# One kept V quarter fewer, and the second MLP split between two places, in a cached-attention decoder on one Trainium2 core

## Chip, cores, metric

The kernel runs on one core of a Trainium2 chip. The metric is the time of one execution in device microseconds, with lower being better. Executions of one kernel spread over about 1.1% here (the kernel before: 1127.4 to 1140.3 us over all rounds; against itself 0.9983 with an interval of 0.996 to 1.0005), so a difference under 0.3% is not told apart by one set of rounds.

## The reference, cut to what matters

There are eight batch rows with one token each. Two layers use the same caches and the same weights.

```python
x = x + _A_ref(_layernorm(x), K, V, wq, wo)      # attention, 16 query heads over 8 K/V heads,
x = x + _B_ref(_layernorm(x), w1, w2, w3, w4)    #   4096 places, 256 wide, in each of 8 rows
x = x + _A_ref(_layernorm(x), K, V, wq, wo)      # again, the same caches
x = x + _B_ref(_layernorm(x), w1, w2, w3, w4)
```

A K or V tile of one row and one head is 2 MB (128 partitions of 16 KB). Read in full for both layers, the 128 K and 128 V tile reads would be 537 MB. The kernel keeps part of a row's K and V on the chip between its two layers. Since the sequence has length one, the shifted parts of `_B_ref` (w1, w2) are zero and what remains is one MLP (w3, w4).

## The kernel before

The program is built from operations with dependencies, and a small list scheduler on the host sets the fixed order of each engine and the place of each load. The tiles are handled in quarters of 512 KB. The buffer has 30 slots of one quarter each.

```python
QUARTERS = 30          # slots of one quarter (4 KB of each partition)
KEEP_K = 5             # heads whose K stays for the second layer: 20 slots
KEEP_V = 4             # quarters of one head's V that stay too
...
def next_kv(i):        # when and where the next load is issued
    ...                # m: 1 to 4 neighbouring quarters of one tile in one load
    late = max(free["sp"], dma_end - self.LEAD)
    ...                # waits for m free neighbouring slots until `late`,
    m = min(m, max(k for k, a in runs(t)))   # then takes what there is
    ...
    q = min(fit) if u.keep else max(fit) + k - m
    return t, m, q
```

The order of work is one loop over the rows. `mid` is the MLP between the two layers of a row; while it runs, the first layer's heads of the next row use their V.

```python
for b in range(B):
    ...
    mid(b, order2[:first])                     # MLP between the layers, queries of layer 2
    run([("b", 0, b + 1, h) ...free heads])    # P.V of the next row's first heads
    if b < B - 2:
        run(both(1, b, order2))                # layer 2 of this row
        run(both(0, b + 1, kept_heads, ...))   # layer 1 of the next row, heads that are kept
    ...
    else:                                      # the last row
        k = both(1, b, l2_heads, ...)
        run(k[:MLP_AT])
        urge[0] = 0
        mlp(x3T[:, :, :], "x3all", B, xoT[:, :, :], ["xo"])   # second MLP, rows 0 to 6, in a batch
        result(B - 1)                                         # their output
        urge[0] = CH
        run(k[MLP_AT:] + ...)
mlp(x1c[B % 2], ("x3", B - 1), 1, xoT[:, :, 0:1], ["xo"])     # second MLP of the last row: the end
result(1)
```

One `mlp` is the sums of the norm, 56 matmuls with w3, 70 with w4, and some 25 small DVE steps.

## Time and profile before

| reading | value |
|---|---|
| time, median of 4 runs | 1131.13 us (1128.87 to 1132.88; 1129.86 of the first 3) |
| span of the first profile | 1124.7 us (a second profile: 1129.4 us) |
| bytes on the load queue | 446.80 MB |
| rate where nothing holds it back | 424 GB/s |
| rate at the turns between rows | 377 to 402 GB/s over 55 us |

I call "turn" the stretch in which a row goes from its first to its second layer. A row's turn is the window from 15 us before to 40 us after DVE writes `x1c` (the row after the first attention), and what it loses is 55 us x (1 - rate / 424 GB/s). The sum over the first seven rows is "the turns' loss" below; the eighth turn is counted by itself, as the last row follows it. (The recorded expectations below quote losses from earlier counts over other windows, such as 28.2 us where this measure gives 24.5; compare them only among themselves.) Here are three of the seven windows, from the stretches of the first profile (columns: window, length, busy time and count of PE, weight loads, DVE, ACT and POOL, granted clock, DMA share, GB/s):

```profile
115.00:170.00 55.00, 45.40 (x1094) 31.50 (x1092) 22.32 (x98) 5.72 (x27) 4.53 (x12) 0.91 1.02 393
...
785.00:840.00 55.00, 45.44 (x1076) 34.18 (x1076) 24.49 (x100) 7.72 (x31) 4.53 (x12) 0.94 0.99 391
918.00:973.00 55.00, 43.38 (x1083) 31.06 (x1083) 23.76 (x100) 7.33 (x33) 4.94 (x13) 1.00 1.00 398
```

The DMA share is near 1 in all of them although the rate is 6 to 8% under the plateau, so the share alone does not show the dip. The rate does.

### The profile page before, as it was taken

How to read it: one execution, taken by the hardware profiler on the slowest of the kernel's cores; microseconds unless marked ns; L12 is line 12 of the kernel's file. 1: busy time of each engine (PE TensorE's matmuls, PEld its weight loads, DVE VectorE, ACT ScalarE, POOL GpSimd, SP SyncE). 2: the span in 40 equal slices, each digit the busy share in tenths (PEclk: the TensorE clock that was granted, in tenths of full speed). 3: DMA queues.
4: the chain of work that ended last, by engine and by line, in shares of the span. 5: the costliest groups of instructions: out<-in, count | busy, mean ns of one | idle time of the engine just before them, and what ended most of it. 6: DMA issues, size and time to landing. Idle time of an engine off the chain costs nothing.

```text
span 1124.7 us, 42351 instructions
## 1 busy us (share of the span) xinstructions
PE 959.9 (85%) x19455; PEld 771.8 (69%) x19455; DVE 556.0 (49%) x1749; ACT 275.8 (25%) x839; POOL 98.0 (9%) x273
## 2 busy tenths in 40 slices
PE   5888888898789989798898987989878988898887
PEld 4677557785678757687677855777666975676775
DVE  4345435455365544454455543655534554456444
ACT  1133012341123302243023411233012430132120
POOL 0001010010100101010010101001010010110010
PEclk9899899899899999999899998899999999999888
DMA  9999999999999999999999999999999999999993
GB/s 334 408 424 421 389 397 424 422 421 382 419 425 423 415 379 422 423 425 408 393 425 423 421 387 409 423 425 420 371 412 426 424 417 374 426 420 398 365 336 132
DMA packets 59570, 449.50 MB, mean 400 GB/s; under 512 B 6384, under 2 KB 9600, under 8 KB 34688
## 3 DMA queue, kind: packets, MB, share of 16 engines
q1 hardware_dynamic: 59392, 446.80, 97.5%
q8 instruction: 152, 2.49, 0.9%
q14 instruction: 26, 0.21, 0.0%
HBM read 446.77 MB, written 0.01 MB: 397 GB/s over the span
## 4 chain that ended last, share of the span: by engine, by line
PE 53%; DMA 35%; DVE 5%; issue 5%; SPq 1%; POOL 0%; ACT 0%
DMA kv<-in_A_k_cache_dram 23%; PE psT L1067 21%; PE psS L915 15%; DMA kv<-in_A_v_cache_dram 11%; PE psP L970 8%; PE psR L1017 3%; PE psM L771 2%; PE psT L1231 1%; DVE oS L982 1%; DVE oS L984 1%; DMA w3x_sb<-in_B_w_dram 1%; PE psP L992 1%; PE psM L868 1%; PE psM L871 1%; SPq L571 1%
## 5 line engine op out<-in xcount | busy, mean ns | idle before, releaser
L1067 PE MATMUL psT<-ident_f,kv 128*128 128x128 f32 x2816 | 398.4, 288 | 32.1 <-DMA kv<-in_A_k_cache_dram 28.9
L1075 DVE COPY kv<-psT 128x512 f32<-128x512 f32 x388 | 267.1, 691 | 214.9 <-PE psT L1067 213.9
L1067 PEld LDWEIGHTS psT<-ident_f,kv 128*128 128x128 f32 x2816 | 320.2, 147 | 54.2 <-DMA kv<-in_A_k_cache_dram 35.4
L1076 ACT COPY kv<-psT 128x512 f32<-128x512 f32 x316 | 184.9, 586 | 407.6 <-PE psT L1067 407.6
L970 PE MATMUL psP<-kv,pT 128*2 128x256 bf16 x4096 | 168.2, 278 | 26.0 <-DMA kv<-in_A_v_cache_dram 15.1
L940 ACT ACTIVATE pT<-sS,nb 128x32 bf16<-128x32 f32 x256 | 81.7, 326 | 332.1 <-DVE nb L934 332.0
L915 PE MATMUL psS<-q2T,kv 128*128 128x48 bf16 x4096 | 141.9, 187 | 20.2 <-issue 19.3
L915 PEld LDWEIGHTS psS<-q2T,kv 128*128 128x128 bf16 x4096 | 126.3, 99 | 44.0 <-issue 39.4
L915 PEld LDWEIGHTS psS<-q1T,kv 128*128 128x128 bf16 x4096 | 136.9, 98 | 14.4 <-issue 9.6
L915 PE MATMUL psS<-q1T,kv 128*128 128x48 bf16 x4096 | 145.7, 184 | 0.9 <-issue 0.9
L970 PEld LDWEIGHTS psP<-kv,pT 128*2 128x2 bf16 x4096 | 79.2, 82 | 63.9 <-issue 25.9
L932 POOL PARTITION_ALL_REDUCE gm<-pm x128 | 45.6, 356 | 792.2 <-DVE pm L930 792.2
L927 DVE COPY sS<-psS 128x64 f32<-128x64 f32 x128 | 28.7, 224 | 120.7 <-PE psS L915 116.3
L992 PE MATMUL psP<-sel,oS 128*128 128x2 bf16 x512 | 32.2, 166 | 48.6 <-DVE oS L984 44.0
L982 DVE CAST oS<-psP 128x256 bf16<-128x256 f32 x128 | 53.9, 421 | 38.7 <-PE psP L970 35.6
L992 PEld LDWEIGHTS psP<-sel,oS 128*128 128x128 bf16 x512 | 24.4, 99 | 68.4 <-DVE oS L984 62.8
L1017 PE MATMUL psR<-wo_sb,oT 128*1 128x448 bf16 x448 | 65.4, 375 | 5.1 <-DVE oT L998 4.9
L944 POOL PARTITION_ALL_REDUCE Db<-rs x128 | 51.2, 400 | 202.2 <-ACT pT L940 202.2
L984 DVE TENSOR_TENSOR oS<-psP,oS 128x256 bf16<-128x256 f32 x128 | 54.2, 423 | 3.2
L1231 PE MATMUL psT<-ident_b 128*128 128x512 bf16 x162 | 54.4, 416 | 0.0
L940 ACT ACTIVATION_READ_ACCUMULATOR pT<-sS,nb 128x1 f32 x256 | 48.1, 188 | 0.0
L771 PEld LDWEIGHTS psM<-x2c,wq_sb 128*128 128x128 bf16 x768 | 30.3, 98 | 21.7 <-issue 17.1
(126 smaller groups left out, 505.7 us busy)
## 6 DMA issues: line engine op xcount, KB each, us to landing
kv<-in_A_k_cache_dram SPq DMA_DIRECT2D x71, 2048.0 KB, 21.7
kv<-in_A_v_cache_dram SPq DMA_DIRECT2D x51, 2048.0 KB, 19.2
kv<-in_A_v_cache_dram SPq DMA_DIRECT2D x171, 512.0 KB, 7.6
kv<-in_A_v_cache_dram SPq DMA_DIRECT2D x42, 1024.0 KB, 12.1
kv<-in_A_k_cache_dram SPq DMA_DIRECT2D x9, 1536.0 KB, 16.0
kv<-in_A_v_cache_dram SPq DMA_DIRECT2D x7, 1536.0 KB, 15.0
kv<-in_A_k_cache_dram SPq DMA_DIRECT2D x21, 512.0 KB, 8.8
kv<-in_A_k_cache_dram SPq DMA_DIRECT2D x10, 1024.0 KB, 14.5
```

The costliest lines, as they stand in the source:

```text
L771: last = t.matmul(bank[:, at + i * step:at + i * step + copies], w, r, start=(kc == 0), stop=(kc == 3))
L915: last = t.matmul(ps[:, 2 * i:2 * i + 2 * REP], a[:, c:256:2], bcast(rhs(c), REP, 1), start=(c == 0), stop=(c == 1))
L940: return a.activation(pT[nr][:, :, :].rearrange("p i j -> p j i")[:, jj, :], sview[:, jj, :], ACT.Exp, bias=nb[nm][:, jj:jj + 1], scale=IN ...
L970: last = t.matmul(ps[g4:g4 + 2, PV0:PV0 + DH], pT[nr][:, i, :], slot_ap(q, s * 256, 256), start=(i < 4), stop=(i >= 28), skip_group_check= ...
L982: plan.op("dve", lambda v: v.tensor_copy(oS[:, 0, :], po), 0.36, "o", rd=[("pv", par, x) for x in range(4)], wr=["oS0"], banks=[bk], prio=hi)
L984: plan.op("dve", lambda v: v.tensor_tensor(oS[:, 1, :], po, oS[:, 0, :], ALU.subtract), 0.36, "o", rd=["oS0"] + [("pv", par, x) for x in r ...
L992: last = t.matmul(ps[:, PV1 + 2 * c:PV1 + 2 * c + 2], oS[:, w, c:DH:2], sel[:, :], start=(w == 0), stop=(w == 1))
L1017: last = t.matmul(psR[r:r + 1, 0:D], oT[no][:, i % 2, i // 2:i // 2 + 1], wo_sb[:, a:a + D], start=(k == 1 and i < 2), stop=(k == HKV - 1 ...
L1067: last = t.transpose(psT[bank][:, s * P:(s + 1) * P], src, ident_f[:, :])
L1075: return e.tensor_copy(dst, psT[bank][:, :])
L1076: return e.copy(dst, psT[bank][:, :])
L1231: return t.matmul(psT[bank][:, :], ident_b[:, :], bcast(ident_b[:, :], 4, 1), start=True, stop=True)
```

## The change

It has four parts: three V quarters kept instead of four, so that one more slot is free while the buffer is fullest; the second MLP of rows 0 to 5 as a batch inside the seventh row's first layer, and that of rows 6 and 7 together at the end; a longer lead from issue to transfer in the scheduler's model; and a placing rule, by which a quarter goes next to the one before it when it fits.

```diff
-KEEP_V = 4
+KEEP_V = 3
-MLP_AT = 3
+MLP_ROW, MLP_AT = 5, 9
-    ISSUE, LEAD = 3.5, 6.0
+    ISSUE, LEAD = 4.0, 6.0
...
+            before = sp_next[i - 1].unit if i else None
+            if before is not None and before.tile is u.tile:
+                for k, a in fit:
+                    if a <= before.slot + 1 <= a + k - m:
+                        return t, m, before.slot + 1
...
+    def with_first_results(k, b):
+        if b != MLP_ROW:
+            return run(k)
+        run(k[:MLP_AT])
+        urge[0] = 0
+        mlp(x3T[:, :, :], "x3all", B - 2, xoT[:, :, 0:B - 2], [("xo", 0)])
+        result(B - 2, 0)
+        urge[0] = CH
+        run(k[MLP_AT:])
...
-            run(k[:MLP_AT])
-            urge[0] = 0
-            mlp(x3T[:, :, :], "x3all", B, xoT[:, :, :], ["xo"])
-            result(B - 1)
-            urge[0] = CH
-            run(k[MLP_AT:] + [("b", 1, b, h) for h in free_heads])
-    mlp(x1c[B % 2], ("x3", B - 1), 1, xoT[:, :, 0:1], ["xo"])
-    result(1)
+            run(k + [("b", 1, b, h) for h in free_heads])
+    mlp(xf, "xf", 2, xoT[:, :, B - 2:B], [("xo", B - 2)])
+    result(2, B - 2)
```

Left out are the lines that make `sums`, `moments`, `norm` and `mlp` take a number of rows. The first output can no longer wait for the end: its row buffer shares bytes with the MLP buffers that later rows need, so the load queue (which is in order) carries it amid the loads.

## The prediction

> **What bounds the kernel now.** I read the slices of the page first, then the queues, then the waits of the load queue, then the stretches.
>
> ```profile
> DMA  9999999999999999999999999999999999999993
> GB/s 334 408 424 421 389 397 424 422 421 382 419 425 423 415 379 422 423 425 408 393 425 423 421 387 409 423 425 420 371 412 426 424 417 374 426 420 398 365 336 132
> ...
> q1 hardware_dynamic: 59392, 446.80, 97.5%
> ```
>
> The DMA row is full, but the GB/s row has two levels: about 424 for most of the time, and a dip to 371-397 once in every batch row, some 130 us apart. The last three slices fall to 365, 336 and 132. So the plateau is the transfer rate, and the kernel loses time where it cannot keep that rate. 446.80 MB at 424 GB/s is 1053.8 us; the span is 1124.7 us, so 70.9 us are lost. To place them I asked for the stretches (columns: window, its length, then busy time and count of PE, weight load, DVE, ACT, POOL; granted clock; DMA share; GB/s).
>
> ```profile
> 0.00:20.00 20.00, 6.62 (x65) 6.16 (x66) 8.01 (x34) 1.28 (x1) 1.18 (x17) 1.00 0.88 353
> 20.00:60.00 40.00, 33.78 (x666) 26.17 (x664) 12.96 (x38) 7.33 (x21) 2.29 (x6) 0.91 1.02 385
> ...
> 829.00:920.00 91.00, 79.67 (x1494) 68.32 (x1493) 47.45 (x126) 30.68 (x87) 9.07 (x24) 0.96 1.01 422
> 880.00:925.00 45.00, 41.72 (x790) 37.03 (x788) 25.16 (x62) 19.86 (x54) 4.94 (x13) 1.00 1.01 421
> 1033.00:1054.00 21.00, 19.02 (x475) 13.12 (x468) 11.90 (x58) 0.22 (x1) 0.00 (x0) 0.84 0.95 354
> 1054.00:1066.00 12.00, 9.12 (x200) 8.70 (x197) 3.97 (x15) 3.20 (x11) 1.51 (x4) 0.86 1.02 398
> 1066.00:1093.00 27.00, 24.12 (x531) 20.20 (x527) 13.84 (x55) 6.01 (x22) 3.02 (x8) 0.81 0.93 317
> 1093.00:1105.00 12.00, 9.04 (x234) 7.13 (x238) 5.09 (x18) 2.61 (x10) 1.51 (x4) 1.00 1.02 416
> 1105.00:1125.00 20.00, 16.13 (x315) 9.71 (x307) 9.17 (x37) 0.22 (x1) 0.00 (x0) 0.79 0.03 11
> ```
>
> The loss of a window is its length times (1 - rate/424). Start: 3.3 + 3.7 = 7.0 us. Last row, 1033 to 1105: 3.5 + 0.7 + 6.8 + 0.2 = 11.2 us. After the last load: about 19.5 us with no traffic, the closing chain. The seven turns between rows, read in the same way from one window each (391 GB/s over 55 us, 397 over 50, 391 over 45, 396 over 45, 396 over 50, 388 over 50, 391 over 45), lose 4.3, 3.2, 3.5, 3.0, 3.3, 4.2 and 3.5: 25.0 us. Together 62.7 of 70.9; the rest is scattered small change in slices of 415 to 422.
>
> Why a turn dips shows in what the load queue waits for, and in its sizes at one turn (780 to 840 us):
>
> ```profile
> SPq L588 <- PE psS L915: 442.6, 102, 25.1
> SPq L588 <- PE psP L970: 424.5, 163, 21.5
> ```
>
> ```profile
> kv<-in_A_v_cache_dram SPq DMA_DIRECT2D x23, 512.0 KB, 8.1
> ```
>
> The queue waits almost always for a matmul of scores or of P·V to give up a quarter of the 30-quarter buffer. At a turn, 20 K quarters and 4 V quarters are kept for the second layer, so 6 are left to stream through: 6 times 524 KB is 3.1 MB in the air or being read. Six windows of 3 us from 793 to 811 us have 350, 381, 306, 391, 300 and 386 GB/s, 352 in the mean; at that rate one pass of a slot takes 3.15 MB / 352 = 8.9 us, of which 8.1 us is the time from issue to landing. The turn is short of slots, not of queue.
>
> **What the Trainium skill says.** "DMA: Bandwidth & Descriptors", Where 436 GB/s comes from, gives a fabric ceiling of 435.2 GB/s; the plateau of 424 agrees (the same page's 358 per core is not what binds here). The same page, Anatomy of one DMA, puts a fixed cost of about 2 us on each DMA (for the other issuing path), mostly the receipt of the last byte: with 1.24 us of transfer per quarter, a lone quarter would need some 3.3 us (an estimate from that page), so most of the 8.1 us here is queueing behind the other quarters; no run shows a lone one yet. "TensorE: Matmul & The Clock Gate", What's actually happening, says that the clock halves after an idle window of about 3.4 us; the trace has 0.50 granted at 1045-1051 and 1075-1081 us, in the last row, so matmul work there costs up to double. "VectorE: DVE Perf Modes", The DRAIN you can't avoid, advises to count instructions, not to fuse; the closing chain's dependent DVE steps do follow one another every 0.20 us at 128x2.
>
> **The change, part by part.**
>
> 1. *Three V quarters kept.* 8 rows each fetch one quarter again: 8 x 0.524 MB = 4.2 MB, at 424 GB/s **+9.9 us** of transfer. In return a turn has 7 streaming slots instead of 6. By the pass time above, 7/6 of 352 is 411 GB/s if a pass stays 8.9 us; a turn's mean of 387 to 397 could thus reach the plateau. But PE too is busy there with the row's MLP and queries, and a slot that waits for a matmul is not helped by a neighbour. Of the 25.0 us of turns plus the 3.5 us of 1033-1054, which is the eighth turn, I take 60% as recovered: **-17.1 us**. This fraction is my choice, and the largest uncertainty.
>
> 2. *The batch leaves the last row.* In its own timeline it is on PE from 1065.1 to 1079.8 us: sums 0.29 + 0.95, first layer 1.47, second layer 0.75 + 0.70 + 1.47, output transposes 0.62, so 6.2 us busy, plus a 1.1 us "issue" gap in the middle of its second layer; DVE adds some 22 small steps of about 0.2 us. The stretch 1066-1093 has PE busy 24.1 of 27 us and only 317 GB/s: here PE, partly at half clock, holds the loads back, which is the 6.8 us loss. Without the batch most of it should go: **-5.5 us**.
>
> 3. *The batch enters the seventh row's first layer* (its place in program order is among the kept heads, around 880-925 us). With 6 rows it has 28 + 56 + 70 + 4 matmuls instead of 36 + 56 + 70 + 4, near 5 us at full clock. PE is busy 41.7 of 45 us there and 79.7 of 91 in the wider stretch, at 421-422 GB/s: it has room for most of 5 us, the loads run 20 us ahead. **+1.5 us**.
>
> 4. *The closing MLP does two rows.* It is the path that sets the end (1114.9 to 1123.2 us). Added: 4 matmuls of sums (0.1), one more variance step (0.2), a second t_h (0.3), a second hidden-layer step (0.25), two base steps (up to 0.2 beside the others), wider gelu steps (0.05). The first layer's 56 matmuls and the second's 70 stay the same in number and width (24 and 12 columns). **+1.1 us**.
>
> 5. *Issue lead 3.5 to 4.0, next quarter next to the last one.* These move only the static order and the placement: more 1-2 MB loads, fewer 512 KB ones. Loads of 512 KB ran at 408-433 GB/s where they were plentiful, so size alone is worth little. **0**, give or take 3.
>
> Sum: 9.9 - 17.1 - 5.5 + 1.5 + 1.1 = -10.1. 1129.9 - 10.1 gives **1120 us**.
>
> **Rivals.** (a) *The slot is not what limits the turn; PE's chain is.* For: PE is 78-85% busy in the seven turn windows and has its gaps there. Against: the queue never stops waiting for slots and 8.1 of 8.9 us are transfer and its queue. Then item 1 recovers perhaps 5 us and the whole is +2: 1132 us. (b) *The first output takes the place of the batch as a wait.* Its row buffer shares bytes with the MLP buffers, and the loads queue is in order, so the output must go out amid the loads (12 places on) and must land before DVE turns the seventh row's sums at about 927 us, as DVE stalls behind that wait. The batch comes some 35 us earlier, so I expect it done; if not, one stall of 5-10 us: 1126-1130. Against it: the order is built with this dependency in view. (c) *The turns close wholly.* Then 28.5 recovered instead of 17.1: 1108 us; the last row's 11.2 then also shrinks to PE's own limit.
>
> **Range and chances.** The recovered share from 20% to 95% gives 1131 to 1110; the last row's 2 to 8 us and the placement's 3 add to both sides. Range 1108 to 1132. Faster by over 2% means below 1107.3, which needs rival (c) and more: 0.07. Slower by over 2% needs 23 us, two stalls of a kind that I do not see: 0.02. Within 2%: 0.91.
>
> **What would show it.** 451.0 MB on the load queue, V issues of 512 KB fewer. Turns at 405-420 GB/s instead of 388-397: item 1; if they stay under 395, rival (a). No sums of eight rows near 1065 us, and the stretch before the last load above 380 GB/s: item 2. The batch's matmuls near 890 us with the rate still at 415 or more, and the turn of the seventh row no later: item 3; a gap on DVE before the cast of the row sums there: rival (b). The end of loads to the end of the kernel 20.5-21.5 us: item 4. The prediction is wrong if the turns stay dipped or if the added traffic is fully paid.

## The result

The changed kernel takes 1131.26 us in the median (1130.45 to 1132.41), the kernel before 1131.13 us in the same rounds; the ratio is 1.0003 with an interval of 0.998 to 1.0026. The record has no mark of correctness for this run itself; `after_keep4` and `after_noadj`, which differ from it by one constant or one rule, are marked correct. Nothing was gained. 10 us of gain had been forecast.

The slices and the load queue of the changed kernel:

```profile
GB/s 342 407 424 421 389 397 426 422 420 382 408 423 424 400 374 420 425 422 415 380 423 424 423 396 399 424 425 420 394 407 425 423 390 385 418 424 414 364 408 153
...
q1 hardware_dynamic: 60544, 450.99, 97.9%
```

The traffic is what was forecast, 451.0 MB, but the dips are all still there. The same three turns in the changed kernel:

```profile
116.00:171.00 55.00, 45.76 (x1040) 28.93 (x1029) 20.11 (x92) 4.64 (x26) 4.12 (x11) 0.84 1.01 394
...
792.00:847.00 55.00, 45.23 (x1058) 30.87 (x1056) 23.81 (x100) 6.56 (x32) 4.92 (x13) 0.91 1.01 400
928.00:983.00 55.00, 44.59 (x1056) 31.54 (x1056) 23.22 (x99) 6.79 (x29) 4.88 (x13) 0.90 1.01 394
```

The turns' loss is 25.2 us in the changed kernel. It is 24.5 us in the first profile of before and 29.4 us in its second, so the first was a lucky one (its span of 1124.7 us is below every timed median too). The load queue still waits for the same two kinds of matmul (waits of the load queue: total, times, longest):

```profile
SPq L596 <- PE psS L947: 467.6, 102, 24.8
SPq L596 <- PE psP L1002: 392.1, 168, 22.4
```

A single-quarter V load of the sixth turn (787 to 847 us) now takes 9.4 us from issue to landing:

```profile
kv<-in_A_v_cache_dram SPq DMA_DIRECT2D x25, 512.0 KB, 9.4
```

The prediction quotes 8.1 us for the corresponding turn of before; the second profile of before has 7.3. Over all seven turns (windows from 20 us before to 40 us after `x1c`), the turns' medians for these loads are 8.4 us in the mean, against 7.6 and 7.4 in the two profiles of before. There is one slot more to six, and the time from issue to landing grew with it. That undoes the arithmetic of the forecast and is the subject of the experiments.

The last row did become shorter. Writes of `x1c` by DVE (start, duration, line, operation, tiles, idle before it) tell the rows apart. In the kernel before, they are the sixth, seventh and eighth row's, the second MLP's input of the last row (the fourth line), and the last copy before the output:

```profile
800.07 0.17 DVE L1051 TENSOR_TENSOR x1c<-acc,psM 128x5 bf16<-128x5 f32 x1 [0.83 <-PE psM L871]
933.17 0.17 DVE L1051 TENSOR_TENSOR x1c<-acc,psM 128x5 bf16<-128x5 f32 x1 [1.01 <-PE psM L871]
1036.36 0.17 DVE L1051 TENSOR_TENSOR x1c<-acc,psM 128x5 bf16<-128x5 f32 x1 [1.26 <-PE psM L871]
1114.65 0.17 DVE L1051 TENSOR_TENSOR x1c<-acc,psM 128x5 bf16<-128x5 f32 x1 [1.32 <-PE psM L871]
1122.83 0.38 DVE L1093 COPY o_row<-psM 1x448 bf16<-1x448 bf16 x1 [0.73 <-PE psM L1089]
```

In the changed kernel the same five, the fourth of which now writes `xf`:

```profile
807.27 0.17 DVE L1083 TENSOR_TENSOR x1c<-acc,psM 128x5 bf16<-128x5 f32 x1 [1.60 <-PE psM L903]
943.26 0.17 DVE L1083 TENSOR_TENSOR x1c<-acc,psM 128x5 bf16<-128x5 f32 x1 [0.83 <-PE psM L903]
1047.20 0.17 DVE L1083 TENSOR_TENSOR x1c<-acc,psM 128x5 bf16<-128x5 f32 x1 [0.85 <-PE psM L903]
1119.15 0.17 DVE L1083 TENSOR_TENSOR xf<-acc,psM 128x5 bf16<-128x5 f32 x1 [0.85 <-PE psM L903]
1128.11 0.38 DVE L1125 COPY o_row<-psM 2x448 bf16<-2x448 bf16 x1 [0.92 <-PE psM L1121]
```

From the eighth row's `x1c` to the end of the span it is 88.4 us before and 82.9 us after. The stretch from the last attention to the copy of the output grew from 8.2 to 9.0 us. The seventh row, from the sixth `x1c` to the seventh, grew from 133.1 to 136.0 us. So the kernel gained at the end and paid earlier: the eighth row's `x1c` comes 10.8 us later than in the first profile of before and 6 us later than in the second (1041.2).

### The profile page after: what moved, and what is told of

It is laid out like the page before. It is cut to its first block, busy times and chain, and to the rows that moved or that the text cites. A ratio compares the mean times of both kernels' runs of the same rounds, so it can differ in the third digit from the quotient of the medians.

```text
span 1130.1 us, 42402 instructions
## 1 busy us (share of the span) xinstructions
PE 971.3 (86%) x19466; PEld 771.2 (68%) x19466; DVE 552.3 (49%) x1749; ACT 278.3 (25%) x844; POOL 97.6 (9%) x275
## 4 chain that ended last, share of the span: by engine, by line
PE 51%; DMA 37%; issue 5%; DVE 5%; POOL 1%; ACT 0%; SPq 0%; POOLq 0%; DVEq 0%
DMA kv<-in_A_k_cache_dram 25%; PE psT L1099 19%; PE psS L947 14%; DMA kv<-in_A_v_cache_dram 13%; PE psP L1002 8%; PE psR L1049 3%; PE psM L797 2%; PE psT L1268 2%; DVE oS L1016 1%; DVE oS L1014 1%; PE psP L1024 1%; PE psM L900 1%; PE psM L903 1%; PE psM L813 1%; ACT pT L972 0%
## 5 line engine op out<-in xcount | busy, mean ns | idle before, releaser
L1099 PE MATMUL psT<-ident_f,kv 128*128 128x128 f32 x2816 | 394.4, 286 | 29.0 <-DMA kv<-in_A_k_cache_dram 27.6
L1107 DVE COPY kv<-psT 128x512 f32<-128x512 f32 x383 | 263.9, 691 | 207.9 <-PE psT L1099 206.5
L1108 ACT COPY kv<-psT 128x512 f32<-128x512 f32 x321 | 188.1, 587 | 416.0 <-PE psT L1099 416.0
L1002 PE MATMUL psP<-kv,pT 128*2 128x256 bf16 x4096 | 181.4, 291 | 19.8 <-DMA kv<-in_A_v_cache_dram 12.5
L972 ACT ACTIVATE pT<-sS,nb 128x32 bf16<-128x32 f32 x256 | 81.9, 327 | 323.5 <-DVE nb L966 323.4
L947 PEld LDWEIGHTS psS<-q1T,kv 128*128 128x128 bf16 x4096 | 136.4, 97 | 14.4 <-issue 10.2
L1268 PE MATMUL psT<-ident_b 128*128 128x512 bf16 x177 | 59.6, 410 | 0.0
L797 PEld LDWEIGHTS psM<-x2c,wq_sb 128*128 128x128 bf16 x768 | 30.3, 98 | 21.5 <-issue 15.8
```

The lines of the kernel that those rows point to most:

```text
L797: last = t.matmul(bank[:, at + i * step:at + i * step + copies], w, r, start=(kc == 0), stop=(kc == 3))
L947: last = t.matmul(ps[:, 2 * i:2 * i + 2 * REP], a[:, c:256:2], bcast(rhs(c), REP, 1), start=(c == 0), stop=(c == 1))
L972: return a.activation(pT[nr][:, :, :].rearrange("p i j -> p j i")[:, jj, :], sview[:, jj, :], ACT.Exp, bias=nb[nm][:, jj:jj + 1], scale=IN ...
L1002: last = t.matmul(ps[g4:g4 + 2, PV0:PV0 + DH], pT[nr][:, i, :], slot_ap(q, s * 256, 256), start=(i < 4), stop=(i >= 28), skip_group_check= ...
L1099: last = t.transpose(psT[bank][:, s * P:(s + 1) * P], src, ident_f[:, :])
L1107: return e.tensor_copy(dst, psT[bank][:, :])
```

## Experiments

The theory after the result (A): the fourth V quarter's traffic, 8 x 0.524 MB at 424 GB/s = 9.9 us, is paid in full, and the seventh slot gives little or nothing at the turns. The rival (B): the slot gives back what I forecast, and another part of the change eats it. All ratios below are to the kernel before in the same rounds; 0.001 is 1.1 us. The table has the readings of the main profiles; the last two columns are the time from the sixth to the seventh `x1c` and from the eighth `x1c` to the end.

| kernel | slots at a turn | MB | turns' loss, us | eighth turn, us | ratio (interval) | seventh row, us | from eighth row, us |
|---|---|---|---|---|---|---|---|
| before, two profiles | 6 | 446.8 | 24.5, 29.4 | 7.3, 7.3 | 1, 0.9983 (0.996-1.0005) | 133.1, 133.0 | 88.4, 88.2 |
| after | 7 | 451.0 | 25.2 | 5.3 | 1.0003 (0.998-1.0026) | 136.0 | 82.9 |
| after_keep4 | 6 | 446.8 | 30.7 | 4.8 | 0.9956 (0.9933-0.998) | 136.6 | 81.5 |
| before_keep3 | 7 | 451.0 | 24.8 | 4.4 | 1.0015 (0.9992-1.0037) | 136.4 | 89.3 |
| before_split | 6 | 446.8 | 28.8 | 6.2 | 0.9955 (0.9921-0.9988) | 136.9 | 83.5 |
| split_again | 6 | 446.8 | 30.1 | 7.1 | 0.9958 (0.9929-0.9987) | 137.9 | 80.6 |
| split_keep3 | 7 | 451.0 | 25.7 | 4.3 | 0.999 (0.9957-1.0023) | 139.9 | 83.7 |
| after_noadj | 7 | 451.0 | 25.0 | 5.2 | 0.9975 (0.9946-1.0005) | 137.5 | 80.6 |
| before_q29 | 5 | 446.8 | 41.9 | 8.7 | 1.01 (1.0065-1.0136) | 137.5 | 90.0 |
| after_q29 | 6 | 451.0 | 28.5 | 5.1 | 1.003 (1.0003-1.0058) | 135.8 | 80.4 |
| after_keep2 | 8 | 455.2 | 16.1 | 5.3 | 1.0018 (0.9969-1.0067) | 137.4 | 83.2 |

### The parts alone

`after_keep4`: the changed kernel with four quarters.

```diff
-KEEP_V = 3
+KEEP_V = 4
```

> The changed kernel with four V quarters kept again. Theory A (the extra quarter of traffic is paid in full, 8 x 0.524 MB at 424 GB/s = 9.9 us, and the seventh slot gives nothing back, as the seven turns lost 28.2 us before and 28.5 us after): 1121 us, 1% faster than before. Theory B (my prediction's: the seventh slot gives back more than it costs, and another part of the change eats it): 1131 or slower, up to 1138. The turns' loss stays 27 to 30 us under A; above 30 under B.

Measured: 1128.91 us, 0.9956. The quarter costs 0.0047 of the time in the changed kernel, 5.3 us. That is half of what A in its strict form said, so something came back. B is out by the time, as it had this kernel at 1131 us or slower. By the other sign that was named, B's would have been a turns' loss above 30 us; it was 30.7 against 25.2 with seven slots, which again says that the slot gives a part back.

`before_keep3`: that part alone.

```diff
-KEEP_V = 4
+KEEP_V = 3
```

> The kernel before with three V quarters kept and nothing else changed. Theory A: 1141 us (+9.9). Theory B: at or below the time of before (1124 to 1131). A schedule that simply shuffles makes either fuzzy by 2 to 3 us.

Measured: 1134.18 us, 1.0015. It is 2 us slower, within noise of nothing. It is neither 1141 (A) nor a clear gain (B): again a part of the 9.9 us comes back, and the interval does not exclude all of it.

`before_split`: the changed kernel with `KEEP_V = 4`, `ISSUE = 3.5` and without the placing rule, so the split MLP alone.

> The kernel before with the split MLP alone (rows 0 to 5 inside the seventh row, the last two at the end), four V quarters, issue lead 3.5, no placing beside the last quarter. From the traces: last row with closing chain lost 31.3 us before and 23.9 after, the stretch ahead of the eighth turn about 1 us more: 1124 us (-6 to -7). If the gain of the last row comes from the seventh slot instead, the time stays at 1131.

Measured: 1127.38 us, 0.9955, a gain of 5 us. Against `before_again` of the same rounds (below) it is only some 3 us, which is not clear of noise by itself; `split_again` repeats the 5 us in other rounds. As this kernel and `after_keep4` have the same ratio, the two small parts add nothing that shows at four quarters.

`before_again`: the kernel before, unchanged.

> The kernel before once more, for its profile and the noise: its profiled run took 1126.6 us where its other runs took 1129 to 1133. Ratio 1.000 within 0.002; a span 3 to 6 us above 1124.7 if that profile was a lucky one.

Measured: 1131.15 us, ratio 0.9983, span 1129.4 us. The first profile was lucky by some 4 us, most of it in its turns.

### The value of a slot, with the traffic held

`before_q29` and `after_q29` have a buffer of 29 slots; nothing else changes against the kernels before and after.

```diff
-QUARTERS = 30
+QUARTERS = 29
```

> The kernel before with a buffer of 29 quarters, so 5 stream at a turn instead of 6, at the same traffic. Slots theory of my prediction (rate in proportion to slots: 5/6 of some 390 GB/s is 325 over 7 turns of 50 us): turns lose about 40 us more, 1170 us. Weak-slots theory (what one more slot gave: some 4 us in the seven turns and 2 in the last): 1136 to 1142 us.

Measured: 1143.39 us, 1.01. The slot from five to six is worth 11 us, 13.2 of them at the turns (41.9 against the mean of 28.7 over the eight profiles named below the next fence). In the stretches, the sixth turn of this kernel:

```profile
796.00:851.00 55.00, 45.34 (x1043) 29.96 (x1041) 23.25 (x98) 6.12 (x31) 4.91 (x13) 0.88 0.95 370
```

PE is as busy as in the kernel before (45.34 against 45.44 us), the rate is 370 instead of 391, and here the DMA share falls too. The proportion that I had forecast with (5/6 of the rate) would have given 1170 us.

The eight profiles with six slots at a turn and the chain as it is: the two of before, `after_keep4`, `before_split`, `split_again`, `after_q29`, `before_pitch` (32.2) and `before_twice` (25.2). Their mean loss is 28.7 us, with a spread from 24.5 to 32.2. The four with seven slots have 24.8 to 25.7, mean 25.2.

> The changed kernel with 29 quarters: three V quarters kept but 6 streaming slots as before, so only the traffic of the change is left of that part. Weak-slots theory: its turns lose 32 us as those of before, 1136 to 1138 us (about 5 over the changed kernel). If the seventh slot gave nothing, 1131 us.

Measured: 1135.42 us, 1.003. This is the cleanest reading of the change's first part. Against `after_keep4` (same six slots, more traffic, other rounds) it is 0.0074 slower, 8.4 us, close to the 9.9 us that the traffic should cost. Against the changed kernel (same traffic, one slot less) it is 0.0027 slower, 3.1 us: that is the slot. Each difference carries some 4 us of noise by the two intervals: the 8.4 is clear of it, and the 3.1 by itself is not. The slot's part rests on the turns' losses of the profiles, 28.7 against 25.2 us in the mean.

`after_keep2`: the changed kernel with two quarters kept, eight slots.

```diff
-KEEP_V = 3
+KEEP_V = 2
```

> The changed kernel with two V quarters kept: 8 slots stream at a turn, 455.2 MB. Turns lost 45 us with 5 slots, 32 with 6, 28 with 7; falling returns: 25 to 27 with 8. Traffic +9.9, given back 2 to 4: 6 to 8 us over the changed kernel, 1137 to 1139 us. If my prediction's proportion (rate by slots) held, the turns would close and it would be at 1130 or less.

Measured: 1132.20 us, 1.0018. My expectation of falling returns was wrong: the turns lost 16.1 us. The sixth turn here:

```profile
792.00:847.00 55.00, 46.65 (x1066) 32.20 (x1067) 22.96 (x100) 7.62 (x33) 4.94 (x13) 0.91 1.01 403
```

The loss by slots is thus 41.9, 28.7, 25.2 and 16.1 us for five to eight. One slot is worth 13.2, 3.5 and 9.1 us at the turns, 8.6 in the mean (single profiles at both ends). A kept quarter is worth 9.9 us of traffic. From four to two kept quarters the traffic costs 19.8 us and the turns give back 12.6 of them; the ratio rises from 0.9956 to 1.0018, 7 us. Traffic and slots pull against each other, which is why the kernel hardly reacts.

### Why a turn stays slow: the size of a load, the addresses, or the matmul chain

In the packet records of the trace, rows of 16 KB take 0.614 us in the median (427 GB/s over 16 engines) and rows of 4 KB, which single-quarter loads have, 0.159 us (412 GB/s); in the mean 0.173 us (378 GB/s), as some 6% of the small rows take over 0.19 us, mostly when few loads are in flight (at the turns of before, 360 to 375 GB/s with 4 to 6 quarters between issue and landing, 394 to 402 with 9 to 12). That suggested two other causes.

`before_pitch`: every load described in pieces of 4 KB at the same addresses, as a reference for the next run.

```diff
-  src = cache[b, h].rearrange("(m s) d -> m (s d)", m=P)[:, u * 2048:(u + n) * 2048]
+  src = cache[b, h].rearrange("(m w s) d -> m w (s d)", w=4, m=P)[:, u:u + n, :]
```

> The kernel before with every load cut into 4 KB rows, at the same addresses; quarter loads are byte for byte what they were, the larger ones go from rows of 16 KB to rows of 4 KB. By the medians of the traces (16 KB in 0.614 us, 4 KB in 0.159): 15616 rows of 16 KB cost 0.022 us more each over 16 engines, about +21 us: 1150 us. If 4 KB rows are slow of themselves (mean 0.173 us): 15616 x (0.692 - 0.622) / 16 = +68 us, 1190 us or more. Reference for the next run.

Measured: 1132.91 us, 1.0007. It failed as an experiment: the neighbouring pieces were joined again, and the trace has the 59392 packets of before. It serves only as one more profile of before.

`before_contig`: a quarter is one stretch of memory, K and V alike, so the result stays correct.

```diff
-  src = cache[b, h].rearrange("(m s) d -> m (s d)", m=P)[:, u * 2048:(u + n) * 2048]
+  src = cache[b, h].rearrange("(w m s) d -> m w (s d)", w=4, m=P)[:, u:u + n, :]
```

> The kernel before with another assignment of sequence places to partitions, the same for K and V: a quarter is one stretch of 512 KB in memory (row pitch 4 KB) where it was 128 rows of 4 KB at a pitch of 16 KB; rows of 4 KB everywhere, as in the run before. Pace theory (the turns are slow since quarter loads at a pitch of 16 KB run at 378 GB/s whatever is in flight): rows of 4 KB take 0.160 to 0.165 us in the mean, and it is 10 to 20 us faster than the same rows at the old pitch. Slots or size theory: equal to it within 3 us.

Measured: 1157.25 us, 1.0219. Without its reference it cannot be judged as planned, but it has two readings of its own. With rows of 4 KB everywhere, the plateau is 405 to 407 GB/s instead of 422, so small rows cost 4%. And the turns ran at 378 to 398 GB/s, as before (a loss of 29.4 us against 424). With 5 to 8 quarters in flight the small rows ran at 372 to 400 GB/s at the turns, where they ran at 368 to 400 in the kernel before. So the addresses of a quarter load are not what slows the turns. Against its own plateau of 406 GB/s, however, this kernel's turns lost only 13.7 us: this fits a share of the row size in the 28.7 us, though no run isolates it.

`split_pairs`: the split kernel, whose queue waits for two neighbouring slots rather than load a single quarter.

```diff
-  t = max(late, times[0])
+  least = min(m, least)                    # least = 2
+  for t in [max(late, times[0])] + [x for x in times if x > late]:
+      if max((k for k, a in runs(t)), default=0) >= least:
+          break
+  else:
+      return None                          # later, or one quarter if nothing else can run
```

> The split kernel whose turns load V by two quarters or more at a time (the queue waits for two neighbouring slots instead of one): some 40 fewer loads, rows of 8 KB. In the traces rows of 8 KB ran at 410 to 416 GB/s with 4 to 8 quarters in flight, those of 4 KB at 362 to 390 with as many. If the size of a load sets the pace at the turns: turns lose 15 to 22 instead of 32 us, 1112 to 1118 us. If what counts is how much is in flight (the large loads merely fell in better moments): waiting for two slots drains the queue, turns lose as much or more, 1127 to 1137.

Measured: 1134.49 us, 1.0032; the turns lost 38.7 us. In this kernel rows of 8 KB are slow at the turns (354 to 387 GB/s with 2, 4, 6 or 8 quarters in flight, where the packet records are many), where the kernels before had 410 to 416 for such rows. So the row size was not the reason that the small rows looked slow. They are what is loaded while little is in flight. Loading fewer, larger pieces drained the queue and cost 8 us against the split kernel.

`before_nomid` and `after_nomid`: the MLP between the layers is left out, with slots and traffic as they were. Their outputs are wrong, which doesn't matter for the times.

```diff
-        mlp(x1c[b % 2], ("x1", b), 1, src[:, :, 0:1], [("x2", b)])
+        dv(lambda v: v.tensor_copy(src[:, :, 0:1], x1c[b % 2][:, :, 0:1]), rd=[("x1", b)], wr=[("x2", b)])
```

> Wrong result on purpose: the kernel before, the MLP between a row's two layers left out at all eight turns (a copy in its place), traffic and slots as they were. Rival (a) of the prediction (PE's chain, 8.3 us from x1 to x2 with 126 matmuls in it, keeps the slots taken): the seven turns lose under 16 instead of 32 us, 1107 us or less with the closing part unchanged. If the 6 slots alone set the turn's rate: 26 us or more, over 1120.

Measured: 1114.87 us, 0.9841, as a wrong result. The turns lost 21.5 us and the eighth 3.8. The sixth turn:

```profile
782.00:837.00 55.00, 44.91 (x1015) 32.54 (x1015) 23.48 (x87) 7.80 (x33) 4.91 (x13) 0.94 1.00 403
```

Taking this MLP away removes 7 of 28.7 us. The chain of matmuls at a turn has a part, but three quarters of the loss stay with six slots and without the MLP (the second layer's queries stay in the chain).

> Wrong result on purpose: the changed kernel without the MLP at the eight turns. It has 7 slots. If chain and slots both count, its turns lose less than the other's without the MLP, by some 3 to 5 us, and with 9.9 us more traffic and the split's 5 us gain it is 0 to 3 us slower than that one. If the chain is all, equal turns, and 5 us slower.

Measured: 1121.78 us, 0.9907. Its turns lost 15.3 us, so the seventh slot is worth 6.2 us without the MLP (one profile each) and 3.5 with it: both count, and each seems to be worth more without the other's limit. It was 7 us slower than `before_nomid`, more than expected; the spans differ by 2.8 us only, so a part of that is the spread of executions.

### What the batch costs in its two places

`before_twice`: the batch done twice in the last row (the line `mlp(x3T...)` doubled).

> The kernel before with the batch of the second MLP done twice at its place in the last row (same result). If matmul and chain work there is paid in full, as the end lost 7.7 us (gross) with the batch and not without: 7 to 8 us more, 1139 us. If the gain of the split came from elsewhere (the order, the second output): 1131 to 1134.

Measured: 1138.23 us, 1.0064, 7 us; and from the eighth row's `x1c` to the end 94.4 instead of 88.3 us. Work there is paid in full.

`split_twice`: the batch of rows 0 to 5 doubled in its new place.

> The kernel before with the split MLP, the batch of rows 0 to 5 done twice inside the seventh row (same result). If that stretch has room for matmul work while the loads run ahead: 1 to 2 us over the split kernel (1127), so 0.996 to 0.998 of before. If work there is paid as in the last row: 5 to 6 us over it, 1.001 of before.

Measured: 1133.58 us, 1.0033 (0.9989 to 1.0077), too wide to judge, and it was repeated beside the split kernel.

> The split kernel once more, so that it stands in the same rounds as its double: 0.9955 of before within 0.003; the seventh row's period (x1 of the sixth row to x1 of the seventh) 137 us against 133 without the batch.

Measured: 1128.43 us, 0.9958, the gain of the split again.

> The split kernel with its batch twice, once more beside the split kernel. If the second pass is paid as the traces say (seventh row's period 137 with one pass, 143.5 with two): 6 to 7 us over the split kernel, 1.001 to 1.002 of before. If the wide interval of its first timing hid a smaller cost: under 3 us.

Measured: 1136.62 us, 1.0031, 8 us over the split kernel; the seventh row took 145.0 instead of 137.9 us. I had read this as matmul work that is paid. The trace says otherwise. Waits of the load queue between 900 and 950 us:

```profile
SPq L591 <- PE psS L942: 23.0, 3, 11.8
SPq L1122 <- DVE o_row L1120: 12.5, 1, 12.5
```

The first output stands in the in-order load queue, twelve places on, and the doubled batch is not ready when the queue gets there: no load is issued for 12.5 us. So this run does not measure the room on PE. It shows rival (b) of the prediction in another form. In `before_split`, `split_again` and `after_keep4` that wait was 1.8 us; in the changed kernel there was none at that place.

### The two small parts, and whether the large ones add

`split_keep3` is `before_split` with `KEEP_V = 3`; `after_noadj` is the changed kernel without the placing rule.

> The kernel before with the split MLP and three V quarters kept, issue lead 3.5 and no placing: the two large parts alone. Measured alone, the parts have ratios 1.0015 and 0.9955 (0.9958 again): added, 0.997. The whole change has 1.0003. If the two small parts (issue lead, placing) cost the difference, 0.997 here; if the two large parts simply do not add, 1.000.

> The changed kernel without the placing of a quarter next to the one before it, issue lead 4.0. Together the two small parts changed nothing at four V quarters (0.9956 with them, 0.9955 without). If the placing costs something at three: 0.997 to 0.999; if it helps to join loads: 1.002 to 1.004, with more 512 KB loads than 174 of V; else 1.000.

Measured: 1131.95 us, 0.999, and 1130.28 us, 0.9975. The sum of the large parts alone would be 0.997. The intervals around 0.999, 0.9975 and 1.0003 overlap, and 0.997 is itself a sum of two uncertain ratios, so neither a cost of the small parts nor an interaction is shown. The placing rule did not join loads: 174 single V quarters with it, 174 without.

## Why the prediction was wrong

**Where it failed: the size of one term in item 1.** "7/6 of 352 is 411 GB/s if a pass stays 8.9 us", and from that a recovery of 60%, "**-17.1 us**". The pass did not stay. With more in flight, each load waited longer behind the others (9.4 instead of 7.3 to 8.1 us at the sixth turn). The text had itself said that most of the 8.1 us was queueing, and did not see that this contradicts a fixed pass. The issue, landing and packet records show it slot by slot. In the 15 us after `x1c`, where with six slots more than half of the turns' loss lies, the kernels with 5, 6, 7 and 8 slots had 4.0, 5.1, 5.8 and 7.0 quarters between issue and landing and moved 320, 357, 368 and 397 GB/s (means over the seven turns and over the one, eight, four and one profiles). What is in flight divided by the rate is 6.6, 7.5, 8.3 and 9.3 us: the pass grew with every slot, and the seventh slot raised the rate by 3% and not by a sixth. Measured in place of the 17.1 us: 28.7 - 25.2 = 3.5 us at seven turns and about 1 to 3 at the eighth, some 5 us. Rival (a) had "perhaps 5 us" for this term, and its total of 1132 us is the one that came; that is in part luck, as its reason, the chain, holds for only a quarter of the loss (the MLP of the chain, 7 of 28.7 us).

**What held.** The mechanism of item 1 is right in kind: fewer slots cost (11 us for the sixth) and more slots do raise the turns. The traffic of +9.9 us is borne out by `after_q29` against `after_keep4` (8.4, with some 4 us of noise). One sign of it did not come: the loads of 512 KB did not become fewer (174 for 171 of V).

**Item 2**, -5.5 us for the batch leaving the last row, was somewhat low. The last row from `x1c` to the end, with the closing chain, fell from 88.3 to 81.9 us in the mean over the seven kernels of the table with the split and three or four quarters; adding back about 1 us of closing chain, the batch was worth 7.4 us there. `before_twice` gives 6 to 7. **Item 4**, +1.1 us, measured 0.8 (8.2 to 9.0 us). **Item 3**, +1.5 us, was too low at four quarters: the seventh row took 136.6 to 137.9 us instead of 133, some 4 us. (At three quarters the batch's own cost does not show so: `before_keep3` took 136.4 us there without the batch, the changed kernel 136.0 and `after_noadj` and `split_keep3` 137.5 and 139.9 with it.) PE was full there, as the stretch of the changed kernel shows, and the rate fell from 421 to 416:

```profile
880.00:925.00 45.00, 44.18 (x866) 40.94 (x865) 27.83 (x82) 16.89 (x45) 4.12 (x11) 0.97 1.00 416
```

That loses 0.5 us more than before in this window (0.8 against 0.3). By the packet records, the whole seventh row of the three kernels with the split and four quarters loses 6.9 to 7.5 us against 424 GB/s, where the two profiles of before lose 3.5; 2 to 2.5 us of the extra lie in the last 20 us before its `x1c`. There the first output held the queue for 1.8 us in these three kernels; what the rest is due to was not settled. **Item 5**, zero, stands, for the two together at four kept quarters. Its remark that loads of 512 KB ran at 408-433 GB/s does not hold: rows of 4 KB, as these loads have, ran at 378 GB/s in the mean over the kernel before.

**The sum, with what was measured:** +9.9 of traffic, -3.5 and about -2 at the turns, -5 for the split as a whole (ratios 0.9955 and 0.9958) is -0.6 us, against a measured +0.3 with an interval of 2.6 us on both sides. The split does gain; the fourth quarter gives it away. `after_keep4` and `before_split` beat both kernels, by 0.44%, and are the same within noise.

Two readings of the prediction do not matter for the sum. The lone quarter's time adds up to 3.2 us, not 3.3. And the idle window that it cites for the halved clock is not seen in the trace: the clock fell to 0.50 at 1045.0 us, and the longest gap between matmuls from 1036 to 1045 us is 0.44 us.

**Rival (b)** did not occur in the changed kernel: its first output was issued at 926.2 us (issues of the output: first and last start), and the cast of the row sums, which must wait for it, came at 938.3 us and had waited for PE:

```profile
L1127 SPq DMA_DIRECT2D out_dram<-o_row x2: 268/304/339, 926.2 to 1128.5; - x2
```

```profile
938.30 0.62 DVE L1057 CAST oW<-psR 128x448 bf16<-128x448 f32 x1 [0.37 <-PE psR L1049]
```

**What stays open.** Of 28.7 us at the turns, the MLP in the chain accounts for 7. Small rows can account for up to about 10: 192 single-quarter loads are 100.7 MB, 247 us at 407 GB/s and 237 us at 424 (an estimate from the plateau of `before_contig`). This part no slot gives back unless loads join. The remaining dozen is a shortage of loads in flight by the evidence of the 29-slot and 8-slot kernels, but no run separates the lead from issue to transfer, the order of the matmuls, and the placing of slots within it.

## What to carry to other kernels

When a pipeline waits for buffers, do not scale its rate by the number of buffers: here a seventh buffer to six raised the rate by 3% in the 15 us where buffers were shortest, and the rest went into a longer wait. So measure the slope by taking one buffer away, and by adding one, as the steps need not be equal. A buffer bought with extra traffic has to be priced against that slope; here the steps brought 13.2, 3.5 and 9.1 us at the turns, 8.6 in the mean, and the last two cost 9.9 us each. Work moved off the closing row paid even though the place it went to was not free, but an output placed in an in-order load queue is a stop for every load behind it.

## What the Trainium skill lacked or had wrong

- "DMA: Bandwidth & Descriptors" gives fixed cost and bandwidth of single transfers, but not how much must be in flight to hold the rate of a queue. Here, with at most 5, 6, 7 and 8 quarters of 512 KB to stream through, the turns ran at 370-384, 377-402, 393-402 and 403-412 GB/s (seven windows of 55 us each; six slots: the two profiles of before; seven: the changed kernel), with a plateau of 424; in the 15 us after `x1c` 4.0, 5.1, 5.8 and 7.0 quarters in flight gave 320, 357, 368 and 397 GB/s.
- "DMA: Bandwidth & Descriptors", Why small descriptors are slow, holds joining of descriptors to be worth it only up to 256 B. Row size still counts above that: here rows of 4 KB instead of 16 KB, in loads of the same size, took the plateau from 422 to 405-407 GB/s and the kernel to 1.0219 of its time. No page says that adjacent pieces of a load are joined, as they were in `before_pitch`: 59392 packets with pieces of 4 KB and without (whether by the software or the chip no run shows).
- No page has an example of an output that waits at the head of an in-order load queue; 12.5 us without an issued load in `split_twice_again`, 1.8 us in `before_split`.
